# Windowed attention and a cosine-gated MLP on one core: the normalisation's engines and the list scheduler's table

## The chip, the cores and the metric

One core of a Trainium2 chip runs the whole program. The metric is device time in microseconds (us): the median of three runs of the kernel before is 723.63 us (722.34 to 723.75).

## What is computed

```python
scores = scale * q @ k.T + bias          # bias: -slope(head) * distance
scores = where(is_global | is_local, scores, -1e9)   # 8 global keys, 96 local ones
a = exp(scores - max(scores)); a = a / (sum(a) + 1e-9)
x = concat_heads(a @ v)                  # 4 batches, 8 heads, 768 positions, head width 64
h = x @ w_in; g = h * cos(h)             # 3072 tokens, 512 -> 2048
out = g @ w_out                          # 2048 -> 512
```

## The kernel before

**Attention.** The 3072 tokens are cut into eight chunks of 384, and a chunk has four head pairs. One head pair of one chunk is a unit (`plan_unit`, `plan_values`): 32 in all. A unit's tokens make four tiles of 96 queries; each tile sees 96 keys of its own, 96 before them and 8 global ones, folded into 104 columns. TensorE makes the scores (L521 for the first eight units, L525 for the others). VectorE folds them (L538), and adds the bias and takes the row's minimum (L547). ScalarE takes exp and the row's sum (L572). VectorE adds 1e-9 to the sums (L580) and takes reciprocals (L583). Then the normalisation multiplies each row by its reciprocal. It is planned per *half pair* (two tiles of both heads: four blocks of up to 104 columns), 64 in all. On ScalarE it is four instructions (L596), on VectorE or GpSimd one of 416 columns (L605), or two where the chunk begins a batch and its first tile has only 96 columns (L600). TensorE then transposes the half pair (L669), VectorE masks it (L677, L682), TensorE multiplies by V (L704), and the result is split into a high and a low part, `xh` and `xl` (L253 or L255, then L725).

**The MLP.** It runs in 128 steps of one chunk and one 128-column block `f` of the hidden layer: 12 matmuls of 384 columns into a `ph` bank (L740), then on ScalarE and VectorE `g = h * cos(h)` (L757 turns, L760 angle, L763 cosine, L798 product) and its split (`gh` copy at L253, L255 or L257; `gl` at L807), then 9 matmuls of 512 columns (L751). There are two `ph` banks, so that step s + 2 waits for L798 of step s. The first steps are chunk 0 with f 0 to 7, chunk 1 with f 0 to 15, chunk 0 with f 8 to 15.

**The weights.** Each of the 32 weight halves arrives as 64-bit floats and is converted by six instructions (`plan_weights`): L378 or L380, L385 or L388, L394 or L396, L399, the copy at L253, L255 or L257, and L409.

**What sets the order.** `Plan.run` is a list scheduler that runs before the program is emitted. Every operation has a table of the engines that may do it with a duration in ns for each, what it comes after, the buffers it uses and a due time. The scheduler goes through a modelled time, gives each free engine the ready operation that is due first, and lets an engine leave an operation to another where that one would be done earlier (duration times `WEIGHT`). An operation with `port=True` on VectorE, and any on GpSimd, is not started in the model while another such one runs on the other engine. What comes out is the order on each engine's queue, and which engine does what; on the chip only data dependences are waited for. ScalarE's exp and sine tables exclude each other, and a change costs an ACT_TABLE_LOAD. Into TensorE's gaps of the first 45 us `emit` puts filler matmuls (L1044). `xdue` says when a chunk's `x` is due; for chunks 0 and 1 by `EARLY`, in ns per unit.

Of the kernel before, what the change touches and what calls it, by code (L numbers as in the profile page):

```python
# [27 lines left out]
SLOT = R + G  # L28
# [15 lines left out]
PERIOD = 5200  # L44
LAG = 3.5
MARGIN, EACH = 3.2, 3.2
EARLY = {0: 2500, 1: 7500}
WEIGHT = {PE: 1, ACT: 0.5, DVE: 1.2, POOL: 0.8}

PHASES = [(0, 0, 8), (1, 0, 16), (0, 8, 16)]  # L50
# [182 lines left out]
class Net:  # L233
# [124 lines left out]
    def plan_weights(self, f):  # L358


        nc, p = self.nc, self.plan
        cols = self.w_in.bitcast(U32)[f]
        rows = self.w_out.bitcast(U32)[f * P : (f + 1) * P, :]
        ends = []
        for kind, src, out in (("wi", cols, self.wi), ("wo", rows, self.wo)):
            raw = self.const.tile([P, 512, 2], U32, name="raw", tag=f"{kind}{f}")
            w0, w1 = raw[:, :, 0], raw[:, :, 1]
            wu = Slot("wu", lambda i: self.work.tile([P, 512], U32, name="wu", tag=i))
            box = {}

            def dma(e, raw=raw, src=src):
                nc.sync.dma_start(raw.rearrange("p c w -> p (c w)"), src)


            def wlow(e, raw=raw, w0=w0):
                h = raw.bitcast(I32)[:, :, 0]
                if e == ACT:
                    nc.scalar.activation(h, w0, AF.Copy, scale=7.49 * 2.0**-32)  # L378
                else:
                    self.eng(e).tensor_scalar(h, w0, 7.49 * 2.0**-32, 1.0, op0=ALU.mult, op1=ALU.mult)  # L380

            def wsign(e, raw=raw):
                if e == DVE:
                    h = raw.bitcast(U16)
                    nc.vector.tensor_scalar(h[:, :, 1], h[:, :, 3], 0x8000, None, op0=ALU.bitwise_and)  # L385
                else:
                    h = raw.bitcast(BF16)
                    nc.gpsimd.tensor_scalar(h[:, :, 1], h[:, :, 3], 0.0, 1.0, op0=ALU.mult, op1=ALU.mult)  # L388

            def wbias(e, w1=w1):  # L390

                x = w1.bitcast(F32)
                if e == ACT:
                    nc.scalar.activation(x, x, AF.Copy, scale=2.0**-112)  # L394
                else:
                    self.eng(e).tensor_scalar(x, x, 2.0**-112, 1.0, op0=ALU.mult, op1=ALU.mult)  # L396

            def wjoin(e, w0=w0, w1=w1, wu=wu):
                nc.vector.scalar_tensor_tensor(  # L399
                    wu.tile, w1, 3, w0, op0=ALU.logical_shift_left, op1=ALU.bitwise_or  # L400
                )

            def whigh(e, kind=kind, out=out, wu=wu, box=box):
                out[f] = box["w"] = self.const.tile([P, 2, 512], F32R, name="w", tag=f"{kind}{f}")
                self.copy(e, box["w"][:, 0, :], wu.tile.bitcast(F32))

            def wrest(e, wu=wu, box=box):
                w = box["w"]
                self.eng(e).tensor_tensor(  # L409
                    w[:, 1, :], wu.tile.bitcast(F32), w.bitcast(F32)[:, 0, :], op=ALU.subtract  # L410
                )

            o = p.op({SP: 470}, dma, extra=1460)
            o = p.op({ACT: 620, DVE: 400, POOL: 700}, wlow, [o], port=True)
            o = p.op({DVE: 610, POOL: 1310}, wsign, [o], port=True)
            o = p.op({ACT: 575, DVE: 345, POOL: 655}, wbias, [o], port=True)
            o = p.op({DVE: 605}, wjoin, [o], [wu], port=True)
            o = p.op({ACT: 525, DVE: 335, POOL: 595}, whigh, [o], [wu], port=True)
            ends.append(p.op({DVE: 605, POOL: 1245}, wrest, [o], [wu], port=True))
        return ends  # L420


# [41 lines left out]
    def plan_unit(self, L, pr):  # L464
# [13 lines left out]
        if exact:  # L478
            raw = row()
            src = self.qk[b, c, 2 * pr : 2 * pr + 2]  # L480

            def load(e):
                nc.sync.dma_start(raw.tile[:, k0:], src.rearrange("j p w -> (j p) w")[:, k0:])

            def queries(e):
                x = raw.tile[:, KW:]
                if e == ACT:
                    nc.scalar.activation(x, x, AF.Copy, scale=self.steep[:, pr : pr + 1])
                else:
                    self.eng(e).tensor_scalar(x, x, self.steep[:, pr : pr + 1], 1.0, op0=ALU.mult, op1=ALU.mult)  # L490

            o = p.op({SP: 470}, load, [], [raw], extra=1422 * (QK - k0) // 1000)
            ready = [p.op({ACT: 430, DVE: 270, POOL: 470}, queries, [o], [raw], port=True)]
            heads = [(raw, ready)] * 2
        else:
            heads = [self.plan_split(row(), self.qk[b, c, 2 * pr + j], k0, self.steepness(2 * pr + j)) for j in range(2)]
# [10 lines left out]
        for js, h in [(js, h) for js in (((0, 1),) if exact else ((0,), (1,))) for h in range(0, CT, 2)]:  # L507
# [17 lines left out]
                            nc.tensor.matmul(out, qs[:, m, q0], ks[:, k : k + w], start=m == 0, stop=m == 1)  # L525

            cols = sum(part(t)[1] for t in ts)
            cost = cols * 17 // 10 if exact else cols * 2 * 46 // 100
            so = self.chain("s", p.op(
                {PE: cost}, score, [o for j in js for o in heads[j][1]],  # L530
                list(pss.values()) + [heads[j][0] for j in js[:1]] + [st, tt[h // 2]], mode="rows" if exact else None,
# [1 line left out]
            for j, ps in pss.items():  # L533
                i0 = 1 if lead(h) else 0

                def fold(e, ps=ps, i0=i0):
                    w = ps.tile[:R, i0 * WIN : 2 * WIN].rearrange("p (a w) -> p a w", w=WIN)
                    nc.vector.copy_predicated(w[:, :, :R], self.mine.bitcast(U32)[:, i0:], w[:, :, SLOT:])  # L538

                o = p.op({DVE: 60 + 100 * (2 - i0)}, fold, [so], [ps])  # L540
                for i, t in enumerate(ts):

                    def least(e, i=i, t=t, j=j, ps=ps):
                        w = width(t)
                        at = 2 * t + j
                        v = t if first and t < 2 else 2
                        nc.vector.tensor_tensor_reduce(  # L547
                            tt[t // 2].tile[:, t % 2, j, :w],
                            ps.tile[:R, i * WIN : i * WIN + w],
                            self.dd[:, v, :w],  # L550
                            op0=ALU.add,
                            op1=ALU.min,
                            scale=-(2.0 ** -(2 * pr + j + 1)),
                            scalar=3.0e38,
                            accum_out=st.tile[:, at : at + 1],
                        )

                    ttr.append(((t, j), p.op({DVE: 180}, least, [o, self.masked], [ps, tt[t // 2], st])))

        n2 = 2 * CT  # L560

        def worst(e):
            nc.vector.tensor_tensor(self.worst[:R], self.worst[:R], st.tile[:, :n2], op=ALU.max)

        self.chain("worst", p.op({DVE: 75}, worst, [o for _, o in ttr], [st], due=self.xdue(n, pr)))
        exps = []
        for (t, j), o in ttr:

# [13 lines left out]
        def rec(e):  # L582
            nc.vector.reciprocal(st.tile[:, 2 * n2 :], st.tile[:, n2 : 2 * n2])  # L583

        o = p.op({DVE: 70}, add, exps, [st])
        o = p.op({DVE: 120}, rec, [o], [st])
        u["norm"] = []
        for h in range(0, CT, 2):

            def norm(e, h=h):  # L590
                x = tt[h // 2].tile.rearrange("p t j w -> p (t j) w")
                r = st.tile[:, 2 * n2 + 2 * h : 2 * n2 + 2 * h + 4].rearrange("p (c o) -> p c o", o=1)
                if e == ACT:
                    for i in range(4):
                        w = width(h + i // 2)
                        nc.scalar.activation(x[:, i, :w], x[:, i, :w], AF.Copy, scale=r[:, i])  # L596
                    return
                if lead(h):
                    for a, w in ((0, R), (2, SLOT)):
                        self.eng(e).tensor_tensor(  # L600
                            x[:, a : a + 2, :w], x[:, a : a + 2, :w],
                            r[:, a : a + 2].broadcast_to([R, 2, w]), op=ALU.mult,
                        )
                    return
                self.eng(e).tensor_tensor(x, x, r.broadcast_to([R, 4, SLOT]), op=ALU.mult)  # L605

            u["norm"].append(
                p.op({DVE: 70 + 2 * 2 * SLOT * 104 // 100, ACT: 560, POOL: 100 + 4 * SLOT * 22 // 10}, norm, [o], [tt[h // 2], st], port=True)
            )
        return u  # L610

    def plan_split(self, raw, src, k0, sc):
# [27 lines left out]

        loads = [p.op({SP: 470}, lambda e, a=a: load(e, a), [], [raw], extra=711 * (QK - k0) // 1000) for a in (0, D)]
        w = KW - k0
        q = self.chain("qhigh", p.op({ACT: 370}, qhigh, loads, [raw, qk]))
        q = p.op({DVE: 470}, qrest, [q], [raw, qk], port=True)
        k = self.chain("khigh", p.op(
            {ACT: 50 + w * 427 // 512, DVE: 70 + w * 265 // 512, POOL: 100 + w * 490 // 512},
# [118 lines left out]
    def plan_step(self, s, n, f, a, b):  # L765
# [10 lines left out]
        for kk in range(self.NK):  # L776

            def m1(e, kk=kk):
                self.moe1(ph.tile, *x.tile, f, kk)

            done = self.chain(f"m1 {s}", p.op(
                {PE: 522}, m1, [self.xdone[n, kk], self.wdone[f][0]], [ph, x], due=due + (kk + 1) * 522,
            ))
            if kk == 0:
                self.chain("m1", done)
# [3 lines left out]
        for c0, c1 in pieces:  # L789
# [20 lines left out]
            for t in range(c0 // P, c1 // P):  # L810

                def m2(e, t=t):
                    self.moe2(po[t].tile, *gg.tile, f, t, f == a, f == b)

                o = self.chain("m2", p.op(
                    {PE: 697}, m2, [g, self.wdone[f][1]], [po[t], gg], due=due + int(LAG * PERIOD) + (t + 1) * 697,
                ))
                if f == b:
                    self.plan_store(n, t, po[t], o, b < self.NF - 1, due + int((LAG + 1) * PERIOD))
# [284 lines left out]
```

## Time and profile before

| what | us |
|---|---|
| median of three runs | 723.63 |
| the profiled execution | 723.99 |
| its span, first to last instruction | 722.3 |
| TensorE busy | 697.8 (97%) |
| VectorE busy | 509.9 (71%) |
| ScalarE busy | 489.4 (68%) |
| GpSimd busy | 129.1 (18%) |

The span is what the profile shows; the profiled execution's own time has 1.7 us more around it. Busy shares are means over a start, in which data and weights arrive, and a long stretch behind it that looks different, so the views are best cut by time.

### The profile page before, as it was taken

How to read it: one execution, taken by the hardware profiler on the slowest of the kernel's cores; microseconds unless marked ns; L12 is line 12 of the kernel's file. 1: busy time of each engine (PE TensorE's matmuls, PEld its weight loads, DVE VectorE, ACT ScalarE, POOL GpSimd, SP SyncE). 2: the span in 40 equal slices, each digit the busy share in tenths (PEclk: the TensorE clock that was granted, in tenths of full speed). 3: DMA queues.
4: the chain of work that ended last, by engine and by line, in shares of the span. 5: the costliest groups of instructions: out<-in, count | busy, mean ns of one | idle time of the engine just before them, and what ended most of it. 6: DMA issues, size and time to landing. Idle time of an engine off the chain costs nothing.

```text
span 722.3 us, 13066 instructions
## 1 busy us (share of the span) xinstructions
PE 697.8 (97%) x4481; PEld 603.4 (84%) x4481; DVE 509.9 (71%) x1505; ACT 489.4 (68%) x1267; POOL 129.1 (18%) x170
## 2 busy tenths in 40 slices
PE   7977989999999999999999999999999999999996
PEld 4646768988899888888889888898888888989984
DVE  7898988886875887567774778757775778644332
ACT  7888987677775667577773886657775796644332
POOL 6345445630000211110000121101000120100000
PEclk8897999999999999999999999999999999999998
DMA  8997121022330322213121322203222210001001
GB/s 304 404 351 194 35 58 35 1 57 64 81 96 1 110 61 57 57 51 96 52 61 40 110 61 57 58 0 101 64 67 66 81 56 1 1 1 44 0 1 49
DMA packets 32605, 55.75 MB, mean 77 GB/s; under 512 B 3473, under 2 KB 18193, under 8 KB 32529
## 3 DMA queue, kind: packets, MB, share of 16 engines
q1 hardware_dynamic: 32528, 54.82, 25.4%
q8 instruction: 37, 0.61, 0.4%
q14 instruction: 40, 0.32, 0.1%
HBM read 48.52 MB, written 6.29 MB: 76 GB/s over the span
## 4 chain that ended last, share of the span: by engine, by line
PE 81%; DVE 7%; ACT 5%; issue 1%; DMA 0%; ACTq 0%; DVEq 0%
PE bank L740 34%; PE bank L751 34%; PE bank L704 5%; PE bank L525 5%; PE bank L669 3%; DVE wu L399 2%; DVE w L409 1%; ACT w L253 1%; ACT rr L763 1%; ACT raw L394 1%; DVE gl L807 1%; DVE tt L547 1%; ACT tt L596 1%; DVE bank L538 1%; DVE raw L385 1%
## 5 line engine op out<-in xcount | busy, mean ns | idle before, releaser
L740 PE MATMUL bank<-xh,w 128*128 128x384 f32 x1024 | 297.9, 343 | 4.4 <-DVE rr L798 3.2
L751 PE MATMUL bank<-w,gh 128*128 128x512 f32 x768 | 244.0, 399 | 0.0
L740 PEld LDWEIGHTS bank<-xh,w 128*128 128x128 f32 x1024 | 190.0, 190 | 12.0 <-DVE rr L798 3.6
L740 PE MATMUL bank<-xl,w 128*128 128x384 f32 x512 | 173.8, 339 | 2.7 <-DVE xl L725 2.7
L751 PEld LDWEIGHTS bank<-w,gh 128*128 128x128 f32 x768 | 138.9, 189 | 21.4 <-issue 0.3
L751 PE MATMUL bank<-w,gl 128*128 128x512 f32 x384 | 152.5, 397 | 0.0
L760 DVE SCALAR_TENSOR_TENSOR rr<-rr,bank 128x384 f32<-128x384 int32 x129 | 69.8, 543 | 104.4 <-ACT rr L757 104.3
L757 ACT ACTIVATE rr<-bank 128x384 int32<-128x384 f32 x129 | 62.0, 482 | 118.2 <-PE bank L740 117.8
L763 ACT ACTIVATE rr<-rr,half_pi 128x384 f32<-128x384 f32 x129 | 78.9, 614 | 43.9 <-DVE rr L760 42.7
L798 DVE TENSOR_TENSOR rr<-bank,rr 128x384 f32<-128x384 f32 x129 | 71.0, 552 | 46.7 <-ACT rr L763 45.9
L740 PEld LDWEIGHTS bank<-xl,w 128*128 128x128 f32 x512 | 97.3, 190 | 7.5 <-DVE xl L725 3.3
L572 ACT ACTIVATE tt<-tt,st 96x104 f32<-96x104 f32 (+1 forms) x256 | 94.4, 370 | 9.7 <-DVE st L547 8.2
L751 PEld LDWEIGHTS bank<-w,gl 128*128 128x128 f32 x384 | 72.4, 189 | 16.8
L257 POOL TENSOR_SCALAR ks<-raw 128x408 fp32r<-128x408 f32 (+1 forms) x43 | 24.7, 574 | 301.6 <-PE bank L525 284.3
L807 DVE TENSOR_TENSOR gl<-rr,gh 128x384 fp32r<-128x384 f32 (+1 forms) x115 | 66.7, 580 | 7.7 <-ACT gh L253 5.7
L547 DVE CUSTOM_DVE_ANT_0 tt<-bank,dd 96x104 f32<-96x104 f32 (+1 forms) x256 | 55.5, 257 | 3.0
L253 ACT CAST gh<-rr 128x384 fp32r<-128x384 f32 (+1 forms) x92 | 46.5, 507 | 11.3 <-DVE rr L798 4.6
L704 PEld LDWEIGHTS bank<-pv,v 104*64 104x64 f32 (+1 forms) x960 | 42.7, 140 | 12.8 <-issue 7.1
L596 ACT ACTIVATE tt<-tt,st 96x104 f32<-96x104 f32 (+1 forms) x152 | 44.6, 369 | 8.4 <-DVE st L583 8.1
L525 PEld LDWEIGHTS bank<-ks,qs 128*96 128x96 f32 x384 | 45.9, 162 | 4.7 <-issue 0.3
L704 PE MATMUL bank<-pv,v 104*64 104x96 f32 (+1 forms) x960 | 48.8, 254 | 0.6 <-ACT pv L253 0.6
L538 DVE COPY_PREDICATED bank<-mine,bank 96x192 f32<-96x192 uint32 (+1 forms) x128 | 40.6, 330 | 11.1 <-PE bank L525 8.0
(97 smaller groups left out, 766.5 us busy)
## 6 DMA issues: line engine op xcount, KB each, us to landing
raw<-in_qk_dram SPq DMA_DIRECT2D x48, 224.0 KB
raw<-in_qk_dram SPq DMA_DIRECT2D x48, 198.0 KB
raw<-in_w_in_dram SPq DMA_DIRECT2D x16, 512.0 KB
raw<-in_w_out_dram SPq DMA_DIRECT2D x16, 512.0 KB
out_dram<-oo SPq DMA_DIRECT2D x24, 256.0 KB
v<-in_v_dram SPq DMA_DIRECT2D x16, 240.0 KB
v<-in_v_dram SPq DMA_DIRECT2D x16, 192.0 KB
raw<-in_qk_dram SPq DMA_DIRECT2D x4, 448.0 KB
```

Of the source, the lines that this page charges most:

```text
L253: self.nc.scalar.copy(out, x)
L525: nc.tensor.matmul(out, qs[:, m, q0], ks[:, k : k + w], start=m == 0, stop=m == 1)
L547: nc.vector.tensor_tensor_reduce(tt[t // 2].tile[:, t % 2, j, :w], ps.tile[:R, i * WIN : i * WIN + w], self.dd[:, v, :w], op0=ALU.add, op1 ...
L572: nc.scalar.activation(x, x, AF.Exp, bias=st.tile[:, c : c + 1], scale=-1.0, accum_out=st.tile[:, n2 + c : n2 + c + 1])
L704: nc.tensor.matmul(px.tile[j * D : (j + 1) * D, t * R : (t + 1) * R], vs.tile[:k, t + c, hs][:, j * D : (j + 1) * D], pv[:k, c, o : o + R] ...
L740: self.nc.tensor.matmul(ph[:, :CW], self.wi[f][:, w, kk * P : (kk + 1) * P], xx[:, kk, :], start=kk == 0 and m == 0, stop=kk == self.NK - ...
L751: self.nc.tensor.matmul(po, gg[:, ts], self.wo[f][:, w, :], start=start and m == 0, stop=stop and m == 2)
L757: self.nc.scalar.activation(r.bitcast(I32), ph, AF.Copy, scale=1.0 / TWO_PI, bias=0.25)
L760: self.nc.vector.scalar_tensor_tensor(r, r.bitcast(I32), -TWO_PI, ph, op0=ALU.mult, op1=ALU.add)
L763: self.nc.scalar.activation(r, r, AF.Sin, bias=self.half_pi)
L798: {DVE: dve}, lambda e, r=r, h=h: nc.vector.tensor_tensor(r(), h(), r(), op=ALU.mult), [o], [ph, rr]
L807: self.eng(e).tensor_tensor(g[1][:, cs], r(), g[0].bitcast(F32)[:, cs], op=ALU.subtract)
```

## The change

The normalisation is no longer offered to ScalarE: the branch with four instructions is gone, and VectorE (70 ns and 1.04 ns a column) or GpSimd (850 ns, which was 1015) does a half pair with one instruction (two at a batch's beginning). The durations in the scheduler's table are set anew, most by a few per cent. Three small VectorE operations (`worst`, L563; the 1e-9, L580; the reciprocal, L583) now carry `port=True`. `EARLY` goes from 2500 and 7500 ns to 3000 and 6000. Nothing else is computed in another way; but with the table, the whole order is made anew.

```diff
-EARLY = {0: 2500, 1: 7500}
+EARLY = {0: 3000, 1: 6000}
...
-            o = p.op({ACT: 620, DVE: 400, POOL: 700}, wlow, [o], port=True)
-            o = p.op({DVE: 610, POOL: 1310}, wsign, [o], port=True)
+            o = p.op({ACT: 580, DVE: 500, POOL: 700}, wlow, [o], port=True)
+            o = p.op({DVE: 650, POOL: 1310}, wsign, [o], port=True)
...
-        self.chain("worst", p.op({DVE: 75}, worst, [o for _, o in ttr], [st], due=self.xdue(n, pr)))
+        self.chain("worst", p.op({DVE: 80}, worst, [o for _, o in ttr], [st], due=self.xdue(n, pr), port=True))
...
-        o = p.op({DVE: 70}, add, exps, [st])
-        o = p.op({DVE: 120}, rec, [o], [st])
+        o = p.op({DVE: 85}, add, exps, [st], port=True)
+        o = p.op({DVE: 120}, rec, [o], [st], port=True)
...
             def norm(e, h=h):
                 x = tt[h // 2].tile.rearrange("p t j w -> p (t j) w")
                 r = st.tile[:, 2 * n2 + 2 * h : 2 * n2 + 2 * h + 4].rearrange("p (c o) -> p c o", o=1)
-                if e == ACT:
-                    for i in range(4):
-                        w = width(h + i // 2)
-                        nc.scalar.activation(x[:, i, :w], x[:, i, :w], AF.Copy, scale=r[:, i])
-                    return
                 if lead(h):
...
-                p.op({DVE: 70 + 2 * 2 * SLOT * 104 // 100, ACT: 560, POOL: 100 + 4 * SLOT * 22 // 10}, norm, [o], [tt[h // 2], st], port=True)
+                p.op({DVE: 70 + 4 * SLOT * 104 // 100, POOL: 850}, norm, [o], [tt[h // 2], st], port=True)
```

In the order that comes out, the 64 half pairs go from 38 on ScalarE, 20 on VectorE and 6 on GpSimd to 54 on VectorE and 10 on GpSimd. The changed file is five lines shorter behind the removed branch, so that its L600 is L605 before, and L720, L752, L755, L758, L793, L802 are L725, L757, L760, L763, L798, L807.

The first place is ScalarE ahead of the first cosine (`rr` is a step's working tile, `tt` a half pair's probabilities). Before:

```order
L757 ACTIVATE rr_830<-bank_594 128x384
L757 ACTIVATE rr_834<-bank_610 128x384
L596 ACTIVATE tt_730<-tt_730,st_731 96x104 x4
L596 ACTIVATE tt_768<-tt_768,st_731 96x104 x4
L763 ACT_TABLE_LOAD
L763 ACTIVATE rr_830<-rr_830,half_pi_113 128x384
L763 ACTIVATE rr_834<-rr_834,half_pi_113 128x384
```

Of the change:

```order
L752 ACTIVATE rr_800<-bank_538 128x384
L378 ACTIVATE raw_140<-raw_140 128x512
L752 ACTIVATE rr_805<-bank_593 128x384
L758 ACT_TABLE_LOAD
L758 ACTIVATE rr_800<-rr_800,half_pi_113 128x384
L758 ACTIVATE rr_805<-rr_805,half_pi_113 128x384
L572 ACT_TABLE_LOAD
```

The eight instructions of the normalisation no longer stand between the turns and the table load; one weight instruction (L378) does, and the exps of the next half pair now come behind the cosines, with a table load of their own.

The second place is VectorE at the last unit of chunk 1 (`st` holds its sums and reciprocals). Before, where the normalisation follows on ScalarE:

```order
L399 SCALAR_TENSOR_TENSOR wu_1283<-raw_138 128x512
L409 TENSOR_TENSOR w_1278<-wu_1267,w_1278 128x512
L255 CAST w_1294<-wu_1283 128x512
L628 SCALAR_TENSOR_TENSOR qs_1169<-raw_758,qs_1169 128x384
L580 TENSOR_SCALAR st_1214<-st_1214 96x8
L583 RECIPROCAL st_1214<-st_1214 96x8
L409 TENSOR_TENSOR w_1294<-wu_1283,w_1294 128x512
```

Of the change:

```order
L399 SCALAR_TENSOR_TENSOR wu_1243<-raw_135 128x512
L580 TENSOR_SCALAR st_1139<-st_1139 96x8
L583 RECIPROCAL st_1139<-st_1139 96x8
L755 SCALAR_TENSOR_TENSOR rr_1245<-rr_1245,bank_1177 128x384
L720 TENSOR_TENSOR xl_950<-bank_1222,xh_949 128x384
L600 TENSOR_TENSOR tt_1138<-tt_1138,st_1139 96x416
L600 TENSOR_TENSOR tt_1192<-tt_1192,st_1139 96x416
```

The three weight instructions ahead of the sums are gone from there, and the normalisation stands on VectorE's own queue, behind an angle and the low part of the unit before.

## Rows read from the trace of the kernel before

**Rows 1.** Windows: busy time of each engine in each stretch, granted clock, DMA share.

```profile
core 0: us, PE busy (x) PEld busy (x) DVE busy (x) ACT busy (x) POOL busy (x), PEclk, DMA share, GB/s
0.00:60.59 60.59, 47.47 (x339) 28.87 (x339) 51.67 (x206) 50.42 (x172) 29.39 (x59) 0.88 1.00 353
60.59:115.01 54.42, 51.22 (x345) 42.63 (x346) 49.61 (x113) 46.53 (x108) 24.96 (x24) 0.92 0.27 65
115.01:160.00 44.99, 44.04 (x252) 39.28 (x251) 38.81 (x80) 34.19 (x76) 23.77 (x19) 1.00 0.07 19
160.00:714.30 554.30, 554.29 (x3543) 492.29 (x3542) 369.67 (x1108) 357.05 (x911) 51.02 (x70) 1.00 0.19 52
...
60.59:66.20 5.61, 5.61 (x17) 5.61 (x18) 5.20 (x6) 4.34 (x9) 5.13 (x5) 0.50 0.89 166
...
101.62:108.20 6.58, 6.58 (x50) 4.84 (x50) 5.02 (x10) 5.66 (x13) 1.22 (x1) 0.74 0.23 62
```

**Rows 2.** TensorE's timeline: start, us, instruction, [idle before and its releaser].

```profile
60.59 0.69 PE L740 MATMUL bank<-xh,w 128*128 128x384 f32 x1 [3.21 <-DVE rr L798]
...
85.74 1.44 PE L669 MATMUL bank<-ident,tt 96*104 96x96 f32 x8 [0.40 <-ACT tt L596]
...
101.62 1.11 PE L669 MATMUL bank<-ident,tt 96*104 96x96 f32 x4 [2.48 <-ACT tt L596]
...
154.62 1.44 PE L669 MATMUL bank<-ident,tt 96*96 96x96 f32 x8 [0.95 <-ACT tt L596]
```

**Rows 3.** ScalarE's timeline ahead of the first product of the MLP.

```profile
55.74 2.28 ACT L596 ACTIVATE tt<-tt,st 96x104 f32<-96x104 f32 x8
58.04 1.28 ACT L763 ACT_TABLE_LOAD   x1
59.33 1.12 ACT L763 ACTIVATE rr<-rr,half_pi 128x384 f32<-128x384 f32 x2
```

**Rows 4.** VectorE's groups up to 60.59 us: count, busy us, mean ns, idle before.

```profile
L409 DVE TENSOR_TENSOR w<-wu,w 128x512 fp32r<-128x512 f32 x9 | 7.3, 818 | 0.3 <-ACT w L253 0.3
...
L385 DVE TENSOR_SCALAR raw<-raw 128x512 uint16<-128x512 uint16 x4 | 4.0, 1011 | 0.0
```

**Rows 5.** VectorE's groups from 60.59 to 115.01 us.

```profile
L399 DVE SCALAR_TENSOR_TENSOR wu<-raw 128x512 uint32<-128x512 uint32 x13 | 11.2, 871 | 0.0
L409 DVE TENSOR_TENSOR w<-wu,w 128x512 fp32r<-128x512 f32 x9 | 7.5, 829 | 0.0
L807 DVE TENSOR_TENSOR gl<-rr,gh 128x384 fp32r<-128x384 f32 x8 | 5.7, 706 | 1.6 <-ACT gh L253 1.6
L798 DVE TENSOR_TENSOR rr<-bank,rr 128x384 f32<-128x384 f32 x9 | 5.0, 557 | 1.4 <-ACT rr L763 1.3
...
L580 DVE TENSOR_SCALAR st<-st 96x8 f32<-96x8 f32 x2 | 1.4, 686 | 0.0
...
L605 DVE TENSOR_TENSOR tt<-tt,st 96x416 f32<-96x416 f32 x1 | 0.6, 581 | 0.0
```

**Rows 6.** VectorE's groups from 300 to 600 us.

```profile
L807 DVE TENSOR_TENSOR gl<-rr,gh 128x384 fp32r<-128x384 f32 x51 | 28.1, 551 | 1.0 <-ACT gh L253 0.2
...
L580 DVE TENSOR_SCALAR st<-st 96x8 f32<-96x8 f32 x14 | 2.3, 166 | 0.2
...
L600 DVE TENSOR_TENSOR tt<-tt,st 96x192 f32<-96x192 f32 (+1 forms) x4 | 1.3, 359 | 0.1
```

**Rows 7.** Timelines of VectorE, and of GpSimd (POOL).

```profile
55.31 0.68 DVE L399 SCALAR_TENSOR_TENSOR wu<-raw 128x512 uint32<-128x512 uint32 x1
...
63.95 1.55 DVE L399 SCALAR_TENSOR_TENSOR wu<-raw 128x512 uint32<-128x512 uint32 x1
...
63.72 1.52 POOL L388 TENSOR_SCALAR raw<-raw 128x512 bf16<-128x512 bf16 x1
```

**Rows 8.** The normalisation's group on ScalarE, from 60.59 to 115.01 us.

```profile
L596 ACT ACTIVATE tt<-tt,st 96x104 f32<-96x104 f32 x12 | 3.5, 369 | 2.8 <-DVE st L583 2.8
```

**Rows 9.** The normalisation's group on GpSimd, over the span.

```profile
L605 POOL TENSOR_TENSOR tt<-tt,st 96x416 f32<-96x416 f32 x6 | 5.3, 878 | 20.8 <-DVE st L583 14.5 <-ACT qs L624 6.3
```

More of the change, by code (lines that the diff above doesn't have):

```diff
@@ L413, in plan_weights @@
             o = p.op({SP: 470}, dma, extra=1460)
-            o = p.op({ACT: 620, DVE: 400, POOL: 700}, wlow, [o], port=True)
-            o = p.op({DVE: 610, POOL: 1310}, wsign, [o], port=True)
-            o = p.op({ACT: 575, DVE: 345, POOL: 655}, wbias, [o], port=True)
-            o = p.op({DVE: 605}, wjoin, [o], [wu], port=True)
+            o = p.op({ACT: 580, DVE: 500, POOL: 700}, wlow, [o], port=True)
+            o = p.op({DVE: 650, POOL: 1310}, wsign, [o], port=True)
+            o = p.op({ACT: 580, DVE: 345, POOL: 640}, wbias, [o], port=True)
+            o = p.op({DVE: 600}, wjoin, [o], [wu], port=True)
             o = p.op({ACT: 525, DVE: 335, POOL: 595}, whigh, [o], [wu], port=True)
-            ends.append(p.op({DVE: 605, POOL: 1245}, wrest, [o], [wu], port=True))
+            ends.append(p.op({DVE: 600, POOL: 1260}, wrest, [o], [wu], port=True))
         return ends
@@ L492, in plan_unit @@
             o = p.op({SP: 470}, load, [], [raw], extra=1422 * (QK - k0) // 1000)
-            ready = [p.op({ACT: 430, DVE: 270, POOL: 470}, queries, [o], [raw], port=True)]
+            ready = [p.op({ACT: 520, DVE: 300, POOL: 490}, queries, [o], [raw], port=True)]
             heads = [(raw, ready)] * 2
@@ L527, in plan_unit @@
             cols = sum(part(t)[1] for t in ts)
-            cost = cols * 17 // 10 if exact else cols * 2 * 46 // 100
+            cost = cols * 17 // 10 if exact else cols * 2 * 47 // 100
             so = self.chain("s", p.op(
@@ L538, in fold @@
                     nc.vector.copy_predicated(w[:, :, :R], self.mine.bitcast(U32)[:, i0:], w[:, :, SLOT:])
-                o = p.op({DVE: 60 + 100 * (2 - i0)}, fold, [so], [ps])
+                o = p.op({DVE: 70 + 98 * (2 - i0)}, fold, [so], [ps])
                 for i, t in enumerate(ts):
@@ L556, in least @@
                         )
-                    ttr.append(((t, j), p.op({DVE: 180}, least, [o, self.masked], [ps, tt[t // 2], st])))
+                    ttr.append(((t, j), p.op({DVE: 188}, least, [o, self.masked], [ps, tt[t // 2], st])))
         n2 = 2 * CT
@@ L642, in plan_split @@
         w = KW - k0
-        q = self.chain("qhigh", p.op({ACT: 370}, qhigh, loads, [raw, qk]))
+        q = self.chain("qhigh", p.op({ACT: 410}, qhigh, loads, [raw, qk]))
         q = p.op({DVE: 470}, qrest, [q], [raw, qk], port=True)
@@ L781, in plan_step @@
             done = self.chain(f"m1 {s}", p.op(
-                {PE: 522}, m1, [self.xdone[n, kk], self.wdone[f][0]], [ph, x], due=due + (kk + 1) * 522,
+                {PE: 527}, m1, [self.xdone[n, kk], self.wdone[f][0]], [ph, x], due=due + (kk + 1) * 527,
             ))
@@ L815, in plan_step @@
                 o = self.chain("m2", p.op(
-                    {PE: 697}, m2, [g, self.wdone[f][1]], [po[t], gg], due=due + int(LAG * PERIOD) + (t + 1) * 697,
+                    {PE: 700}, m2, [g, self.wdone[f][1]], [po[t], gg], due=due + int(LAG * PERIOD) + (t + 1) * 697,
                 ))
```

## The prediction

> **What bounds the kernel now.** I read the busy time by stretch first, then TensorE's waits with their timeline, then the two engines that these waits name.
>
> By stretch [rows 1], TensorE is busy for 554.29 of the 554.30 us from 160 us to the last product. No wait is left there, so whatever another engine gains or loses in it is covered by TensorE. The end of the kernel is thus set by when TensorE gets its work in the first 160 us. Up to 60.59 us VectorE (51.67 us) and ScalarE (50.42) are busy for some five sixths of the time, the DMA engines all of it, and TensorE does a few scores, transposes and fillers. From 60.59 to 115.01 us it is fed, but VectorE (49.61 of 54.42 us) and ScalarE (46.53) hardly keep up. From 115.01 to 160 us they have 6 and 11 us to spare.
>
> TensorE's timeline shows where it is late [rows 2]: 3.21 us at 60.59 us for the first product L798, which frees a `ph` bank; 0.40 us at 85.74, 2.48 us at 101.62 and 0.95 us at 154.62 for a transpose's input, each time on ScalarE's normalisation L596. Behind the first the granted clock is 0.50 (1.2 of 2.4 GHz) for 5.61 us, behind the third it is 0.74 on the mean for 6.58 us [rows 1]: some 2.8 and 1.7 us of work lost.
>
> What holds the product at 60.59 us is a chain on ScalarE [rows 3]: eight pieces of normalisation for 2.28 us, a table load of 1.28, the cosine. The transpose at 101.62 us waits for the same L596, but that one waits in turn for the reciprocal: in this stretch L596 stands idle for 2.8 us on L583 [rows 8]. There VectorE is the late one, and part of why is its port: L399 takes 0.68 us alone, and 1.55 us where GpSimd's L388 runs beside it [rows 7].
>
> **The change, part by part.**
>
> *The start of the stream.* The eight pieces ahead of the first cosine are gone (first place of the order): minus 2.28 us on that chain [rows 3]. One L378 has come between the two turns. The second turns wait for three more matmuls anyway, so I count it as nothing; as long as two of the pieces (0.6 us) if they don't. VectorE must be as early: up to the first product it now has three L409 (818 ns), one L385 (1011 ns) and seven smaller instructions less, and six L600 (359 ns) and two L605 (581) more. The seven lie between 0.17 and 0.83 us; at 0.4 that is 2.5 + 1.0 + 2.8 less against 2.2 + 1.2 more, some 2.9 us less in all [rows 4 to 6]. Both engines agree, so **minus 2.3 us** (bounds: 0, if a load or VectorE is late in their place, and minus 2.9). The DMA queue puts one half pair's query load behind one weight more, 0.5 MB, 1.4 us at the stretch's 353 GB/s; that unit's scores are needed long before its values, whose load keeps its place, so it costs nothing; without that cover 1.4 us.
>
> *From there to the last `xl` of chunk 1* (in the stretch that ends at 115.01 us), VectorE paces. In the new order it has four L605 more (2.3 us), two L385 (2.0), three small ones of a further unit (0.17 to 0.69 each, I take 0.4: 1.2), and eight copies, scalings and maskings between 0.36 and 0.83 us (I take 0.5, most being copies: 4.0): 9.5 us. It has four L409 less (3.3), four L807 (2.8), one L399 (0.9) and two L628 (at L807's 0.7: 1.4): 8.4 us. Net **plus 1.1 us** (with the ends of these prices, minus 0.7 and plus 4.6) [rows 4 to 6].
>
> Against it, ScalarE loses 3.5 us of L596 there [rows 8]. VectorE waits 2.9 us for ScalarE's cosines and `gh` copies in this stretch [rows 5]; with ScalarE at 46.5 of 54.4 us I take half of that as gone: **minus 1.4 us** (bounds 0 and minus 2.9).
>
> The port: L399 (13 times 0.19 us over 0.68), L409 (9 times 0.15 over the same), L807 (8 times 0.16) and L580 (2 times 0.52) lose 6.0 us beside GpSimd [rows 5 to 7]. GpSimd now has 19 instructions in this part where it had 24 [rows 1], so I take a fifth off: **minus 1.2 us**. The three `port=True` cost no instruction; they only order the queue. Bounds: the whole 6.0 us gained, or as much again lost.
>
> *The wait at 154.62 us* was for ScalarE too; that half pair now goes to VectorE, which has 6 us to spare there. I take half: **minus 0.5 us** (0 to minus 0.95).
>
> *Behind that.* Some 25 half pairs go to VectorE in the covered stretch, at 0.58 us, or twice 0.36 where there are two: 16 us against 185 us in which VectorE is idle [rows 1, 5, 6]; ScalarE is relieved of as much. The half pairs on GpSimd take 0.88 us [rows 9]. With TensorE full, none of it counts. If VectorE fell behind a unit's transposes there, it would cost that wait and the clock behind it.
>
> Sum: -2.3 + 1.1 - 1.4 - 1.2 - 0.5 = -4.3 us. The profiled execution took 723.99 us, 0.36 more than the median, 723.63; so 719.7 for a profile like it and **719.3 us** for the median.
>
> **The rivals.**
>
> *TensorE is late no more* (0.18). If VectorE keeps up wholly, TensorE also loses its 0.40 and 2.48 us of waits, 1.7 us of clock behind them and the 0.95: with the start, 7.8 us, **715.8 us**; with full clock from the start 2.8 less, 713.0. For it: all four waits of TensorE lead to L596, and the 38 half pairs on ScalarE are gone. Against it: the wait at 101.62 us was VectorE's in the end.
>
> *The gain is given back at the port* (0.14). Norms that ran on ScalarE touched no port of GpSimd; now each can meet it. If the units of chunk 1 lose 1.4 us each in their chain of sums, reciprocal and two norms, the three whose transposes TensorE waits for eat up the 4.3 us: **723.6 us**.
>
> *The norm becomes the late one* (0.18). The same mechanism further on, which decides from 1.4 us a unit. One L399 loses 0.87 us to one L388 [rows 7], and four instructions stand in the chain of a unit: up to 3.5 us, of which 0.5 is paid now (L580 at 686 against 166 ns [rows 5, 6]). In the new order, at the last unit of chunk 1, the two norms also stand behind the low part `xl` of the unit before, which waits for TensorE and ScalarE (second place). At 2.5 us a unit, three units, with one more fall of the clock at 1.7 us: 9.2 - 4.3 = 4.9 us slower, **728.5 us**. Against it: fewer GpSimd instructions, and three weight instructions fewer ahead of the sums. The Trainium skill speaks for this rival (SBUF — State Buffer, "SBUF: two separate sides"): the port pair is an exclusive lock, held for a whole instruction by a GpSimd operation or by a VectorE operation with two SBUF inputs, and ScalarE never waits for it; the norm has two SBUF inputs, so by that rule it moves from an engine that cannot be held up to two that can. The trace agrees on the lock: 1.55 us against 0.68 [rows 7].
>
> **How the numbers follow.** My sum has 0.50; its own range, with each term half way to its bounds, is some 3.5 us to either side. With the first rival, faster by over 0.2% (1.45 us, about what a measurement here can tell from no change) has 0.68; same 0.14; slower 0.18. The range from 712.8 to 726.0 leaves out the worse part of the last rival and the tail of the first, under 0.2.
>
> **What the changed profile would show.** Right: the first L740 behind L793 starts at about 58 us; ScalarE has no ACTIVATE on `tt` but exp; the stretch to the last `xl` of chunk 1 is about 1.5 us shorter; from 160 us TensorE is full. Wrong, if the stream starts at 60 us or later, if TensorE waits for the norm L600 for more than 3 us in all, or if it waits at all behind 160 us. VectorE's mean on L580, L399 and L409 shows the port.

## The result and the profile after

The changed kernel takes **713.74 us** (median of four runs, 711.55 to 714.31) where the kernel before, run beside it, takes 723.39: a ratio of 0.9863 (95% interval 0.9839 to 0.9887). That is 9.7 us faster; the prediction had 4.3, and its range (712.8 to 726.0) holds the time.

The windows of the changed kernel, cut at the same events as the rows of before: the first product of a steady stream, the last `xl` matmul of chunk 1 that TensorE waits for, 160 us, the last product.

```profile
core 0: us, PE busy (x) PEld busy (x) DVE busy (x) ACT busy (x) POOL busy (x), PEclk, DMA share, GB/s
0.00:56.84 56.84, 45.08 (x338) 28.04 (x338) 51.22 (x203) 43.72 (x138) 26.39 (x55) 0.94 0.99 357
56.84:102.49 45.65, 44.77 (x332) 37.58 (x332) 43.23 (x111) 39.31 (x93) 28.76 (x24) 0.96 0.33 84
102.49:160.00 57.51, 55.94 (x318) 49.31 (x319) 51.30 (x113) 43.56 (x94) 28.94 (x23) 1.00 0.13 33
160.00:704.20 544.20, 541.64 (x3493) 482.84 (x3492) 372.96 (x1116) 322.89 (x807) 51.74 (x64) 1.00 0.20 53
...
56.84:61.45 4.61, 4.61 (x17) 4.61 (x18) 4.12 (x11) 4.22 (x13) 1.69 (x2) 0.63 1.07 287
61.45:102.49 41.04, 40.16 (x316) 32.97 (x315) 39.11 (x102) 35.09 (x81) 27.07 (x23) 1.00 0.25 61
```

For the second of them, here is the same cut in the kernel before, which [rows 1] don't have.

```profile
60.59:110.55 49.96, 46.76 (x326) 38.84 (x326) 45.55 (x106) 42.81 (x100) 23.33 (x22) 0.91 0.27 63
```

Read as differences: the stream starts 3.75 us earlier (60.59 to 56.84), the stretch to chunk 1's last `xl` is 4.31 us shorter (49.96 to 45.65), and the rest 2.0 us shorter (110.55 to 714.30 is 603.75, 102.49 to 704.20 is 601.71; some 0.7 of it because one more group of L751 lies ahead of the cut). That sums to 10.1 us, the time between the two last products; the spans differ by 9.9 us (722.3 and 712.4). In the second stretch 2.0 us is TensorE's work running faster (46.76 to 44.77 busy: one fall of the clock to a mean of 0.63, and 1.00 from 61.45 us on) and 2.3 is idle time.

TensorE's timeline at the first two cuts: start, us, instruction, [idle before and its releaser].

```profile
56.84 0.44 PE L735 MATMUL bank<-xh,w 128*128 128x384 f32 x1 [3.70 <-DVE rr L793]
...
102.49 0.44 PE L735 MATMUL bank<-xl,w 128*128 128x384 f32 x1 [0.83 <-DVE xl L720]
```

ScalarE ahead of that first product; it answers to [rows 3].

```profile
52.87 0.47 ACT L752 ACTIVATE rr<-bank 128x384 int32<-128x384 f32 x1
53.24 0.66 ACT L378 ACTIVATE raw<-raw 128x512 int32<-128x512 uint32 x1
53.79 0.47 ACT L752 ACTIVATE rr<-bank 128x384 int32<-128x384 f32 x1
54.28 1.28 ACT L758 ACT_TABLE_LOAD   x1
55.58 1.12 ACT L758 ACTIVATE rr<-rr,half_pi 128x384 f32<-128x384 f32 x2
```

The 2.28 us of pieces are gone from this chain, and VectorE was early enough. The table load starts 3.76 us earlier (58.04 to 54.28), 1.5 more than the pieces, since the turns themselves start earlier. The kernel before had one more wait of TensorE ahead of them. VectorE and TensorE of the kernel before, from 49.8 us:

```profile
49.88 2.15 DVE L409 TENSOR_TENSOR w<-wu,w 128x512 fp32r<-128x512 f32 x2
51.95 1.85 DVE L385 TENSOR_SCALAR raw<-raw 128x512 uint16<-128x512 uint16 x1
53.61 0.52 DVE L725 TENSOR_TENSOR xl<-bank,xh 128x384 fp32r<-128x384 f32 x1
```

```profile
54.18 0.44 PE L740 MATMUL bank<-xl,w 128*128 128x384 f32 x1 [2.37 <-DVE xl L725]
```

And VectorE of the changed kernel, which makes the same `xl`:

```profile
50.82 0.73 DVE L385 TENSOR_SCALAR raw<-raw 128x512 uint16<-128x512 uint16 x1
51.35 0.58 DVE L720 TENSOR_TENSOR xl<-bank,xh 128x384 fp32r<-128x384 f32 x1
```

The low part comes 2.26 us earlier, with one weight instruction ahead of it that takes 0.73 us where it took 1.85.

Over the whole span, TensorE's busy time fell by 9.2 us (697.8 to 688.6) with the same matmuls, and its idle time by only 0.7: the waits below went, others came, and most of the gain lies inside what the profile counts as busy.

TensorE's waits over the whole span, before and after (releaser: us in total, times, longest), tell a different part of it.

```profile
PE bank L669 <- ACT tt L596: 7.7, 6, 2.5
PE bank L740 <- DVE rr L798: 3.2, 1, 3.2
PE bank L740 <- DVE xl L725: 2.7, 2, 2.4
```

```profile
PE bank L735 <- DVE rr L793: 4.3, 2, 3.7
PE bank L664 <- DVE tt L595: 2.6, 2, 2.3
PE bank L664 <- DVE tt L600: 1.9, 5, 1.1
...
PE bank L664 <- POOL tt L600: 0.7, 3, 0.3
```

Before, the largest group is a transpose that waits for ScalarE's normalisation. But the view holds only waits in which TensorE is idle. In the kernel before there is another kind, inside "busy" time. Here are ScalarE and TensorE of the kernel before at 403 to 406 us, two views of one place.

```profile
403.38 2.29 ACT L596 ACTIVATE tt<-tt,st 96x104 f32<-96x104 f32 x8
```

```profile
404.00 0.33 PE L740 MATMUL bank<-xh,w 128*128 128x384 f32 x1
404.17 1.84 PE L669 MATMUL bank<-ident,tt 96*104 96x96 f32 x8
405.80 0.43 PE L740 MATMUL bank<-xh,w 128*128 128x384 f32 x1
```

The eight transposes end (406.01) when ScalarE's last piece has ended (405.67). From the first one's start to the last one's it takes 1.55 us; in 13 of the 24 such groups behind 120 us of the changed kernel the same eight need 0.58. TensorE follows ScalarE piece by piece, and since a matmul lasts longer from its start to its end (0.243 us at least for a transpose) than the step to the next one, each short wait lies inside the time of the matmul before it, and the row has no "[idle before]". Behind 160 us the steps from a transpose to the next sum to 19.1 us before (159 steps) and 14.3 after (155).

I therefore use one figure for all runs below, the **lateness of the transposes**: for each of the 256, the time from the start of the TensorE instruction before it to its own start, less what such a step takes undisturbed (the tenth percentile behind 160 us over all seventeen traces: 0.082 us behind another transpose, 0.173 behind a first-layer and 0.230 behind a second-layer matmul, 0.1 for kinds that do not occur there). It is 20.7 us before and 13.6 after, 7.1 us less where the time is 9.7 less. Of these 7.1 us, 5.2 lie ahead of 160 us, where TensorE's idle waits and its lower clock are part of the figure, and 1.9 behind it.

### The profile page after: what moved, and what is told of

The parts are those of the page before. It is cut to its first block, busy times and chain, and to the rows that moved or that the text cites. A ratio compares the mean times of both kernels' runs of the same rounds, so it can differ in the third digit from the quotient of the medians.

```text
span 712.4 us, 12947 instructions
## 1 busy us (share of the span) xinstructions
PE 688.6 (97%) x4483; PEld 598.4 (84%) x4483; DVE 518.8 (73%) x1542; ACT 450.9 (63%) x1130; POOL 135.8 (19%) x166
## 4 chain that ended last, share of the span: by engine, by line
PE 72%; DVE 11%; ACT 8%; issue 2%; DMA 1%; POOL 0%; ACTq 0%; DVEq 0%; POOLq 0%; SPq 0%
PE bank L735 31%; PE bank L746 30%; PE bank L699 5%; PE bank L525 3%; ACT tt L572 2%; PE bank L664 2%; DVE wu L399 1%; ACT rr L758 1%; ACT L572 1%; DVE w L409 1%; DVE tt L547 1%; DVE gl L802 1%; DVE rr L755 1%; DVE qs L623 1%; DMA raw<-in_qk_dram 1%
## 5 line engine op out<-in xcount | busy, mean ns | idle before, releaser
L746 PE MATMUL bank<-w,gh 128*128 128x512 f32 x768 | 243.6, 398 | 0.0
L746 PEld LDWEIGHTS bank<-w,gh 128*128 128x128 f32 x768 | 138.4, 188 | 21.5 <-ACT raw L394 0.3
L746 PE MATMUL bank<-w,gl 128*128 128x512 f32 x384 | 151.9, 396 | 0.0
L755 DVE SCALAR_TENSOR_TENSOR rr<-rr,bank 128x384 f32<-128x384 int32 x129 | 69.8, 542 | 102.6 <-ACT rr L752 102.2
L752 ACT ACTIVATE rr<-bank 128x384 int32<-128x384 f32 x129 | 62.1, 482 | 127.5 <-PE bank L735 124.5
L758 ACT ACTIVATE rr<-rr,half_pi 128x384 f32<-128x384 f32 x129 | 78.4, 613 | 43.0 <-DVE rr L755 41.4
L793 DVE TENSOR_TENSOR rr<-bank,rr 128x384 f32<-128x384 f32 x129 | 70.5, 551 | 41.2 <-ACT rr L758 40.6
L572 ACT ACTIVATE tt<-tt,st 96x104 f32<-96x104 f32 (+1 forms) x256 | 94.2, 369 | 7.0 <-DVE st L547 6.4
L746 PEld LDWEIGHTS bank<-w,gl 128*128 128x128 f32 x384 | 72.1, 188 | 16.7
L257 POOL TENSOR_SCALAR ks<-raw 128x408 fp32r<-128x408 f32 (+1 forms) x35 | 21.1, 602 | 308.6 <-PE bank L525 291.6
L802 DVE TENSOR_TENSOR gl<-rr,gh 128x384 fp32r<-128x384 f32 (+1 forms) x113 | 65.9, 583 | 7.7 <-ACT gh L253 5.5
L253 ACT CAST gh<-rr 128x384 fp32r<-128x384 f32 (+1 forms) x99 | 50.2, 508 | 29.0 <-DVE rr L793 20.5
L525 PE MATMUL bank<-ks,qs 128*96 128x200 f32 (+1 forms) x384 | 47.9, 255 | 0.5 <-DVE st L547 0.5
L572 ACT ACTIVATION_READ_ACCUMULATOR tt<-tt,st 96x1 f32 x256 | 47.9, 187 | 0.0
```

The lines of the kernel that those rows point to most:

```text
L253: self.nc.scalar.copy(out, x)
L572: nc.scalar.activation(x, x, AF.Exp, bias=st.tile[:, c : c + 1], scale=-1.0, accum_out=st.tile[:, n2 + c : n2 + c + 1])
L746: self.nc.tensor.matmul(po, gg[:, ts], self.wo[f][:, w, :], start=start and m == 0, stop=stop and m == 2)
L752: self.nc.scalar.activation(r.bitcast(I32), ph, AF.Copy, scale=1.0 / TWO_PI, bias=0.25)
L755: self.nc.vector.scalar_tensor_tensor(r, r.bitcast(I32), -TWO_PI, ph, op0=ALU.mult, op1=ALU.add)
L758: self.nc.scalar.activation(r, r, AF.Sin, bias=self.half_pi)
```

## The experiments

Theory P (price): the scheduler's table had 560 ns for a half pair on ScalarE; four pieces take 1.19 us from the start of the first to the end of the last (1.17 to 1.20 over all 38; [rows 3] have two such groups in 2.28). So it put the transposes on TensorE's queue some 0.6 us too early, and everything behind them waited. Theory T (table): the other new numbers bring the gain. Theory L (luck): any new order scatters by several us. A fourth, that four pieces as such are what costs, came with the third run.

The times are medians, each ratio is to the kernel before run beside it (medians of 722.2 to 724.2 us), and differences between two kernels are taken from their ratios, times 723.4.

| kernel | us | ratio to before (95%) | lateness, us |
|---|---|---|---|
| before | 723.4 | 1 | 20.7 |
| after | 713.7 | 0.9863 (0.9839 to 0.9887) | 13.6 |
| e1, norm alone | 719.6 | 0.9943 (0.9923 to 0.9963) | 17.9 |
| e2, the rest alone | 721.2 | 0.9967 (0.9949 to 0.9985) | 21.4 |
| e3, true price alone | 711.3 | 0.9862 (0.9826 to 0.9899) | 8.8 |
| e4, old order, norm on VectorE | 733.5 | 1.0146 (1.0125 to 1.0166) | 28.9 |
| e7, after with ScalarE at its true price | 712.9 | 0.9851 (0.9827 to 0.9875) | 10.1 |
| d1, price half corrected | 713.7 | 0.9868 (0.9840 to 0.9897) | 14.2 |
| d2, after, underpriced | 732.5 | 1.0137 (1.0116 to 1.0159) | 31.2 |
| d3, true price and port rule | 713.1 | 0.9871 (0.9850 to 0.9892) | 9.3 |
| e5, after without port rule | 715.4 | 0.9890 (0.9863 to 0.9916) | 14.4 |
| e6, after with old due times | 718.7 | 0.9940 (0.9919 to 0.9961) | 15.3 |
| e9, after with old durations | 715.0 | 0.9883 (0.9854 to 0.9911) | 13.6 |
| j1, after, meaningless step | 712.4 | 0.9849 (0.9812 to 0.9887) | 12.1 |
| j2, before, meaningless step | 721.7 | 0.9973 (0.9961 to 0.9984) | 19.8 |
| j3, e3, meaningless step | 712.0 | 0.9841 (0.9818 to 0.9864) | 8.6 |
| j4, e1, meaningless step | 717.8 | 0.9938 (0.9915 to 0.9962) | 17.0 |

Over these 17 profiled executions span and lateness go together (correlation 0.97; 1.02 us of span for each us of lateness; the largest miss is 2.7 us). That is a correlation: it doesn't show that the late transposes cost all of the time.

**e1: the normalisation alone.**

```diff
-                if e == ACT:
-                    for i in range(4):
...
-                p.op({DVE: 70 + 2 * 2 * SLOT * 104 // 100, ACT: 560, POOL: 100 + 4 * SLOT * 22 // 10}, norm, [o], [tt[h // 2], st], port=True)
+                p.op({DVE: 70 + 4 * SLOT * 104 // 100, POOL: 850}, norm, [o], [tt[h // 2], st], port=True)
```

> Kernel before with one part of the change: normalisation as one op on VectorE or GpSimd, at their measured prices; every other duration, the due times and the port rule stay as before. Theory P (ScalarE's half pair takes about 1.19 us in four pieces where the plan reckons 0.56, so TensorE's transposes come late or are paced by it, hidden inside busy TensorE): most of the 9.7 us comes with this part, 715 to 718 us, and the start-to-start time of neighbouring transposes behind 160 us falls from 19.1 us in sum to about 14. Theory T (the new durations, due times and port rule bring it): 721 to 724 us, whatever the transposes do. Theory L (any new order scatters by some us): anywhere from 714 to 726, and not in step with the transposes' pace.

719.6 us, between P's and T's. Behind 160 us the transposes' steps fall to 15.6 us, nearly as P said, but TensorE now waits elsewhere. Its waits over the span:

```profile
PE bank L664 <- DVE tt L600: 5.9, 9, 2.9
PE bank L521 <- ACT raw L488: 4.1, 3, 2.4
PE bank L735 <- DVE rr L793: 2.9, 3, 2.2
```

The whole gain is not in this part alone: with the old due times and durations, the normalisation on VectorE comes late, mostly in the first 105 us (the wait of 2.9 us is at 85 us).

**e2: all but the normalisation.**

```diff
 (on the changed kernel; ScalarE's branch with four pieces is back)
-                p.op({DVE: 70 + 4 * SLOT * 104 // 100, POOL: 850}, norm, [o], [tt[h // 2], st], port=True)
+                p.op({DVE: 70 + 4 * SLOT * 104 // 100, ACT: 560, POOL: 850}, norm, [o], [tt[h // 2], st], port=True)
```

> The changed kernel with ScalarE's four-piece normalisation given back at the old price of 0.56 us; the new durations, due times and port rule stay. P: the plan puts some 40 half pairs on ScalarE again, the transposes are paced as before (sum about 19 us), 719 to 723 us. T: 714 to 716 us, as the change. L: anywhere from 712 to 724.

721.2 us, in P's range, with 40 half pairs on ScalarE; the steps behind 160 us sum to 17.8 us (P: about 19), the lateness to 21.4. T falls as the main cause.

**e3: one number.**

```diff
-                p.op({DVE: 70 + 2 * 2 * SLOT * 104 // 100, ACT: 560, POOL: 100 + 4 * SLOT * 22 // 10}, norm, [o], [tt[h // 2], st], port=True)
+                p.op({DVE: 70 + 2 * 2 * SLOT * 104 // 100, ACT: 1190, POOL: 100 + 4 * SLOT * 22 // 10}, norm, [o], [tt[h // 2], st], port=True)
```

> Kernel before with one number changed: the plan's price of a half pair on ScalarE is 1.19 us, as measured, in place of 0.56. ScalarE still takes 31 half pairs. P: the plan now knows when they end, so the transposes are placed later and run at their own pace: 716 to 720 us. If it is the pieces themselves and not their price that cost (each piece frees only a quarter of the transposes): 721 to 723. T: 722 to 724. L: no rule.

711.3 us, better than even P expected: the kernel before with one number put right gains as much as the whole change, with 31 half pairs still on ScalarE in four pieces. The waits of TensorE:

```profile
PE bank L669 <- ACT tt L596: 3.3, 3, 2.3
PE bank L521 <- issue: 3.2, 1, 3.2
PE bank L521 <- DVE raw L490: 2.3, 1, 2.3
```

The wait for L596 is 3.3 us where it was 7.7, and the lateness 8.8 where it was 20.7.

**e4: the old order, the normalisation quicker.** Each half pair that was planned for ScalarE is put out on VectorE, at the same place of the order.

```diff
-                if e == ACT:
-                    for i in range(4):
-                        w = width(h + i // 2)
-                        nc.scalar.activation(x[:, i, :w], x[:, i, :w], AF.Copy, scale=r[:, i])
-                    return
+                if e == ACT:
+                    e = DVE
```

> Kernel before in its very order: where the plan put a half pair on ScalarE, the same place in the order gets one op on VectorE instead. So no new schedule at all, and no scatter from one. P: the transposes are no more paced by pieces; VectorE takes on 38 ops of about 0.56 us that were not reckoned, ScalarE loses 38 of about 1.19: 717 to 721 us. T and L: 723 to 726 us, since the order is the old one and VectorE is the fuller.

All three theories missed the size: 733.5 us, 10.6 slower by the ratio. The operation itself takes about half as long (416 columns on VectorE take 0.58 us at the median of 42, 0.69 on the mean), but it stands in a queue that was not planned for it.

```profile
PE bank L666 <- DVE tt L602: 10.0, 13, 2.9
PE bank L666 <- DVE tt L597: 3.6, 6, 2.1
```

So here a quicker operation on a queue that the plan had not reckoned with is worse than the slow one. What the four pieces cost as such this run doesn't tell; e3 and e7 do.

**Luck.** Three kernels with the price of a group of three first-layer matmuls changed by 1 ns, and e1 the same way.

```diff
-                {PE: 527}, m1, [self.xdone[n, kk], self.wdone[f][0]], [ph, x], due=due + (kk + 1) * 527,
+                {PE: 528}, m1, [self.xdone[n, kk], self.wdone[f][0]], [ph, x], due=due + (kk + 1) * 527,
 (j1, on the changed kernel; j2, j3, j4: 522 to 523, on the kernel before, e3 and e1)
```

> The changed kernel with a number that means nothing: the plan's price of one product of the first layer is 528 ns in place of 527. The order of the work comes out another way, nothing else does. Theory P (what counts is that the plan knows when the normalisation ends): 712 to 716 us, as the change. Theory L (each new order scatters by several us): off the change's 713.7 by more than 3 us, either way.

> The kernel before with the same meaningless step, 523 ns in place of 522; ScalarE's half pair stays priced at 0.56 us. P: 720 to 726 us, as before, with neighbouring transposes behind 160 us at about 19 us in sum. L: off 723 by more than 3 us, either way.

> The kernel before with ScalarE's half pair priced at 1.19 us, and the meaningless step of 523 ns on top. P: 709 to 715 us, as with the price alone (711.3). L: the 711.3 was a lucky order, and this one comes out at 715 to 723.

> Normalisation moved off ScalarE alone (719.6 us), with the meaningless step of 523 ns for 522. If 719.6 was an unlucky order of a change that is worth 10 us by itself: 711 to 716. If moving 38 half pairs to VectorE needs the rest of the change (durations, due times, port rule) to pay: 717 to 722 again.

By the ratios they come out 1.0, 2.0, 1.5 and 0.4 us below their kernels; only j2's 2.0 lies outside the intervals. This is a weaker trial of luck than it was meant to be: counted by kind of instruction, the step moves 9 to 36 of some 4000 instructions on TensorE's queue, while e3's price moves 227. What speaks against L are the orders that do differ. e3, e7, d1 and d3 (the last three stand below) have a price nearer to the truth, and any two of them differ in 121 to 201 instructions of that queue; they take 711.3 to 713.7 us. The kernel before and e2, both with 0.56 us, differ in 160 and take 723.4 and 721.2. So a new order is worth some 2 us among these, not 10. e1's 719.6 looks like no accident either: j4 takes 717.8, and e6 below, with the same due times, 718.7.

**e7: the change with ScalarE back, at the true price.**

```diff
 (on the changed kernel; ScalarE's branch with four pieces is back)
-                p.op({DVE: 70 + 4 * SLOT * 104 // 100, POOL: 850}, norm, [o], [tt[h // 2], st], port=True)
+                p.op({DVE: 70 + 4 * SLOT * 104 // 100, ACT: 1190, POOL: 850}, norm, [o], [tt[h // 2], st], port=True)
```

> The changed kernel with ScalarE's four-piece half pair given back, but at 1.19 us: new durations, due times and port rule stay, 31 half pairs go to ScalarE. P: 709 to 715 us, and 6 us or more below the run with the same half pairs at 0.56 us (721.2). If it is one op instead of four pieces that counts, not the price: 717 to 721. L: anywhere.

712.9 us, 8.4 below e2, from which it differs by that number and by what the plan makes of it (31 half pairs on ScalarE, not 40). So one op in place of four pieces isn't what counts.

**The rest of the change, one part undone at a time.**

```diff
 (e5: port=True taken from worst, add, rec)
 (e6)
-EARLY = {0: 3000, 1: 6000}
+EARLY = {0: 2500, 1: 7500}
 (e9: all durations but the normalisation's as before)
```

> The changed kernel without the port rule on the three small VectorE ops (worst, add, reciprocal). If that rule is what the norm on VectorE needs: 717 to 721 us. If it is worth what the prediction gave it (1.2 us): 714 to 715.5. If nothing, as the 1.5 us scatter of the orders so far would hide: 711 to 715.

> The changed kernel with the old due times of the first two chunks. If the due times are what the norm on VectorE needs: 717 to 721 us, with the stretch from the start of the stream to the last low part of chunk 1 back at 49 us or more. If not: 711 to 715.

> The changed kernel with the old durations of everything but normalisation; new due times and port rule stay. If the recalibrated durations are what the norm on VectorE needs: 717 to 721 us. If not: 711 to 715.

By the ratios the port rule is worth 2.0 us and the durations 1.4, both no more than the scatter of an order; the due times 5.6, beyond it. In e6 TensorE's longest wait for a low part, 2.3 us, is for the last one of chunk 1; the changed kernel waits 0.83 us there, and the kernel before 0.32:

```profile
PE bank L664 <- DVE tt L595: 4.1, 2, 2.3
PE bank L735 <- DVE xl L720: 3.7, 3, 2.3
```

With the normalisation off ScalarE, the due times matter: from the first L751 (L746 in the changed file) to the 73rd it takes 55.5 us in e1 and 53.4 in e6, 52.4 before the change and 48.7 after; where ScalarE keeps 31 half pairs at the true price, they don't (e3 with the old ones 711.3, e7 with the new 712.9).

**Is it the error in the price?** d1 takes half of it away, d2 puts one like it on the changed kernel's one-op normalisation, d3 adds the port rule to e3.

```diff
 (d1, on the kernel before: ACT: 560 becomes ACT: 875)
 (d2, on the changed kernel)
-                p.op({DVE: 70 + 4 * SLOT * 104 // 100, POOL: 850}, norm, [o], [tt[h // 2], st], port=True)
+                p.op({DVE: 236, POOL: 400}, norm, [o], [tt[h // 2], st], port=True)
 (d3: e3, and port=True on worst, add, rec)
```

> The kernel before with ScalarE's half pair priced halfway, 0.875 us for the 1.19 that it takes. If the size of the error in the plan sets the loss: between the two, 715 to 719 us, with the lateness of the transposes (about 21 us in sum before, 9 us at the true price) at 12 to 18. If only the split over the engines matters, or a threshold: at either end, 711 to 713 or 722 to 724.

> The changed kernel with its new normalisation priced at less than half of what it takes, as ScalarE's was before: 0.236 us for 0.50 on VectorE, 0.40 for 0.85 on GpSimd. If it is the plan's error that costs, on whatever engine: the transposes' lateness rises from 14 to 18 or more, 716 to 721 us. If it is the four pieces on ScalarE: no change, 712 to 715.

> The kernel before with the true price of ScalarE's half pair and the port rule on the three small VectorE ops, nothing else of the change. If the port rule's 1.7 us (715.4 without it, 713.7 with it) adds to the price's 12: 708 to 711 us, below both kernels. If what the rule saves is the same late transposes: 710 to 713.

d2 shows that a wrong price costs on another engine too: 732.5 us, 19.8 above the changed kernel, by two wrong numbers alone and with nearly the same split (52 half pairs on VectorE and 12 on GpSimd, 54 and 10 in the changed kernel). TensorE's waits, and its time from 160 us on:

```profile
PE bank L664 <- DVE tt L600: 8.2, 19, 1.3
PE bank L735 <- DVE rr L793: 4.0, 2, 3.5
PE bank L664 <- DVE tt L595: 3.9, 9, 1.0
PE bank L664 <- POOL tt L600: 3.9, 8, 0.9
PE bank L664 <- POOL tt L595: 2.0, 5, 0.5
```

```profile
160.00:722.50 562.50, 551.59 (x3521) 485.86 (x3520) 377.54 (x1130) 326.34 (x806) 63.36 (x76) 1.00 0.19 51
```

18 us of waits for a normalisation in 41 places, 0.44 on the mean, and a stretch from 160 us on in which TensorE idles for 10.9 us. d1 got nearly the whole gain (713.7) for half of the correction: the time lost is not in proportion to the error. Its split is e3's (31 half pairs on ScalarE, 38 before), so the split could be what counts between 560 and 875. The lateness says more: for each half pair that ScalarE normalises it is 0.51 us before, 0.26 in d1 and 0.07 in e3, so from d1 to e3 it follows the price with the split unchanged. What the split alone is worth in time stays open: no run has 31 half pairs on ScalarE at 560. d3's 713.1 is no lower than e3's 711.3: the port rule's gain does not add.

## Why the prediction was right or wrong

*The direction and the range* were right, the range in part by luck: the prediction's own sum with its 3.5 us to either side ends at 715.8, and 713.7 lies inside only because the first rival had stretched the range to 712.8. The size was wrong in three terms, and a fourth, the due times, had none.

*The start of the stream*, minus 2.3 us (bounds 0 and minus 2.9): measured 3.75, beyond the far bound. The eight pieces did leave the chain and VectorE was as early. But I took what stands ahead of the turns as fixed, and read over the wait of 2.37 us at 54.18 us, for an `xl` behind three weight instructions on VectorE; in the new order it is gone.

*The stretch to the last `xl` of chunk 1*, net minus 1.5 us: measured 4.31. **This is the step that failed most.** I took VectorE as what paces it and summed up its instructions (plus 1.1), the waits (minus 1.4) and the port (minus 1.2). VectorE's busy time in the stretch fell by 2.3 us (45.55 to 43.23), where instructions and port had made 0.1 less; but the row of TensorE's waits had the answer: 2.48 us for L596, a fall of the clock behind it, both gone. "The wait at 101.62 us was VectorE's in the end" is what I held against the first rival, from 2.8 us in which L596 stood idle on the reciprocal [rows 8]. That is one reading of the row; the other is that the transpose stood on TensorE's queue too early, because the plan took the four pieces for 0.56 us. e3 speaks for the second: the same pieces, the right price, and the stretch up to the same matmul is shorter still. Between the first L751 and the 73rd I read 52.4 us before, 48.7 after and 46.4 in e3. Nor did the prediction price `EARLY`: with the old due times (e6) the changed kernel takes 53.4 us there, no less than before, so that in the change as it stands this gain needs both parts, the price gone and the due times.

*Behind that*, minus 0.5 us at the wait at 154.62, and 0 from 160 us on. From the 73rd L751 to the last it takes 594.7 us before and 593.5 after, 1.2 less, and in e9 or d2 the same part takes 595.3 and 607.9: it is no covered stretch. "No wait is left there" was read from 554.29 busy of 554.30 us [rows 1]. Busy is from a matmul's start to its end, and steps between transposes 0.08 us apart can stretch to 0.27 without an idle nanosecond showing. The steps lost 4.8 us (19.1 to 14.3), of which new small waits gave part back: TensorE is idle for 2.6 us there now, where it never was, and that was one of the prediction's own signs of being wrong.

*The port*, minus 1.2 us: 2.0 between e5 and the changed kernel, one order against one order, and no gain in d3. It cannot be told from 0.

*The rivals.* The first, "TensorE is late no more" (715.8, 713.0 with full clock), comes nearest; I gave it 0.18. The three waits for L596 that it names are gone, and TensorE waits for no normalisation in the second stretch; but it is still late for the first product, by 3.70 us where it was 3.21. Its reason, that VectorE keeps up, isn't the one that e3 shows. Against it stood one row with two readings, and for it all four waits. The last one, in which the normalisation becomes late behind the port, did not come: in the changed kernel L600 takes 0.863 us on the mean of five in the second stretch; the two longest, 1.65 and 0.87 us, run beside GpSimd's L388, and two with GpSimd idle take 0.58. So the hold is there. The Trainium skill ("SBUF — State Buffer", "SBUF: two separate sides") describes such a hold as an exclusive lock. But TensorE waited for VectorE's normalisation only 1.9 us in five places (L600) and 2.6 us in two (L595), all but 0.4 us of it in the first 36 us. A normalisation that comes late on VectorE shows where the plan is wrong about VectorE, in e4 and d2.

*What I overlooked.* Both numbers stood in what I had read: 560 in the diff's last line, and 2.28 us for two half pairs in [rows 3]. I priced the removed work and never asked what the wrong price did to the work placed behind it.

## What to carry to other kernels

Where a program sets the order, compare its table with the trace line by line before anything else: an operation that takes twice its price can make the engine behind it wait at many places (41 in d2), and one number (e3) was worth as much as the whole change. A quicker operation that the plan doesn't know of can cost more than the slow one (e4). And do not read "100% busy" as "no wait": compare start-to-start steps of equal instructions, since a wait shorter than a matmul's latency has no idle time.

## What the runs showed that I had not expected

- TensorE's busy time is no measure of its work: 697.8 us before, 688.6 after and 687.6 in e3, with the same matmuls. Part of it is the clock in the first 160 us (0.93 on the mean before, 0.97 after, 0.98 in e3), part the paced transposes.
- A step of 1 ns in one price of 522 or 527 moves 9 to 36 of some 4000 instructions on TensorE's queue and the time by 0.4 to 2.0 us. With this scheduler a difference below 2 us between two orders says nothing of the part that was changed.
